# Nine inner blocks beside attention, later use of VectorE's block turns, and the query scale in an eviction

## The chip, the cores and the metric

The kernel runs on one core of a Trainium2 chip. The metric is the device time of one execution in microseconds (us), the median of three runs. TensorE does matrix products and whole 128x128 transposes, VectorE, ScalarE and GpSimd work element by element, and SyncE (SP) issues nearly all DMAs.

## The reference

Attention with a threshold feeds two MLPs in a row, all in float32:

```
scores = (q @ k.T) / 8                        # q, k, v: 4 batches, 8 heads, 576 rows, 64 columns
scores = where(scores >= rowmax - tau, scores, -1e9)
attn   = exp(scores - rowmax) / sum
x      = attn @ v                             # brought to 2304 tokens x 512
h = x @ w_in1;  x = (0 if h <= -1; (h+1)**2/4 between; h if h >= 1) @ w_out1
h = x @ w_in2;  out = (h * clip(h + 3, 0, 6) / 6) @ w_out2     # w: 512 x 2048 and 2048 x 512
```

## The kernel before, in words

**Attention** is 16 jobs, one per batch and pair of heads (`jobs`), each cut into five blocks of query rows (four of 128, one of 64 for both heads). For a block, `em_scores` (L314) multiplies queries and keys into the score banks P0 and P1 in PSUM. VectorE evicts them as minus the scores and takes the row minimum on the way (L341), ScalarE takes the exponential (L353), and VectorE masks and sums (L362). TensorE then turns the result (`em_pt`, L379, through `turn`, L277) and multiplies it with the values (`pv_chunk`, L413). `pre_norm`, `fetch_norm` and `em_norm` bring the row sums round through DRAM and scale the result on GpSimd (L481).

**Turning queries and keys** (`unit_q`, L281, and `unit_k`, L296). Before a job its queries and keys are turned so that the head's columns lie on the partitions. There are two forms, chosen by the job's number and `JT`. For jobs below `JT` the rows are loaded as they are, TensorE turns five and six blocks of 128 into a score bank, and ScalarE evicts each of the two (L294, where the queries are multiplied by 0.125, and L309). From `JT` on the DMAs place the rows in strips of 32 (`strips`, L222), and VectorE's transpose of 32x32 squares finishes the turn in SBUF (L286, L302); GpSimd then multiplies the queries by 0.125 (L288). Both forms end by issuing the load for the next job.

**The first MLP beside attention.** The 2048 inner columns of each MLP are 16 blocks of 128. Once the first batch's attention is done (`ready(0)`), `dense1` (L803) runs the first `NF1` inner blocks for the first three batches, in groups of 256 tokens. `ROUNDS` (L782) lists the groups and their inner blocks: the first two groups go in two rounds each, with half of the blocks a round, since the weights come in meanwhile; the second round adds what the first has stored. `em_h` (L657) is one inner step, 12 matmuls of 256 columns, and `em_part` (L712) half of its output, six. A loop at the end of the kernel runs attention as a generator: each of its pauses adds `share` to a credit (L927, L941), which pays for pieces of `dense1` at 0.33 each; so the pieces stand between those of attention in TensorE's order.

**Weights.** Every block of a weight is loaded and split into a high and a low part for exact products (`split_a`, `split_b`, L111 to L143): passes on ScalarE, VectorE and GpSimd (L122, L137, L141). `pace` and `ahead1` (L915, L920) ask for the splits by the inner step at which they are first used.

**Behind attention** `dense` (L835) runs the first MLP for the fourth batch and the tails with all 16 blocks, then the other three batches with the blocks from `NF1` on (`fs2`), in steps of 512 tokens (`em_h` again, and `em_out`, L693), and then the second MLP. `taus` (L886 to L888) holds four columns: the threshold as used, the factor 0.125, the threshold as given, and one for intermediate use.

Of the kernel before, what the change touches and what calls it, by code (L numbers as in the profile page):

```python
# [11 lines left out]
ALU = mybir.AluOpType  # L12
# [6 lines left out]
def kernel(  # L19
# [13 lines left out]
    V, S, G, T = nc.vector, nc.scalar, nc.gpsimd, nc.tensor  # L33
# [7 lines left out]
    HS = SEQ // 2  # L41
# [3 lines left out]

    WIDE = [MAIN] * NB + [NB * TAIL]
    NW = len(WIDE)
    NF1 = 10
    NAT = 1
    JT = 4  # L50
    MLAG = 2
    RAW = 3
    MORE = 2
# [10 lines left out]
    taus = const.tile([128, 4], F32, name="taus")  # L64
# [6 lines left out]
    def narrow(t, g):  # L71
        return t[g // 2][:, :, (g % 2) * GRP:(g % 2 + 1) * GRP]
# [29 lines left out]
    def after(ins, prev, sync=False):  # L102
        if prev is not None:
            kind = mybir.DependencyClass.Sync if sync else mybir.DependencyClass.NoSync
            why = mybir.DependencyReason.ANTI if sync else mybir.DependencyReason.DATA
            tc.add_manual_dep(ins.ins, prev.ins.name, mybir.DependencyInfo(kind, why), reason="pace")
# [4 lines left out]
    def split_a(kind, m, f):  # L111
        t = wraw.pop((kind, m, f))
        pool = wbase if f < NF1 else wpool[f]
        hi = pool.tile([128, 512], F32R, tag=f"w{kind}h{f}", name=f"w{kind}h{f}")
# [97 lines left out]
    qt, kt = {}, {}  # L212
# [4 lines left out]
    def rows(src, b):  # L217
        if b >= NAT or JT < HP:
            return src[0:MAIN, :].rearrange("(c p) d -> p c d", c=4)
        return src[0:MAIN, :].rearrange("(p c) d -> p c d", c=4)  # L220

    def strips(t, s0, src, h):  # L222
        n = src.shape[0] // 32
        flat = t.rearrange("p c n -> p (c n)")
        for x in range(2):
            p0 = 64 * h + 32 * x
            nc.sync.dma_start(out=flat[p0:p0 + 32, 32 * s0:32 * (s0 + n)].rearrange("p (s d) -> p s d", d=32),  # L227
                              in_=src[:, 32 * x:32 * x + 32].rearrange("(s p) d -> p s d", p=32))

    def load_q(j):  # L230
        if j >= NJ:
            return
        E = nc.sync if j else nc.scalar
        b, hp = jobs[j]
        for h in HEADS:
            src = q[b, 2 * hp + h]
            if j >= JT:
                strips(qn, 0, src, h)
                continue
            E.dma_start(out=qn[:, 0:4, h * D:(h + 1) * D], in_=rows(src, b))  # L240
            E.dma_start(out=qn[0:TAIL, 4, h * D:(h + 1) * D], in_=src[MAIN:SEQ, :])

    def load_k(j):
# [3 lines left out]
        for h in HEADS:  # L247
            src = k[b, 2 * hp + h]
            if j >= JT:
                strips(kn, 2, src, h)  # L250
# [18 lines left out]
    def unit_bank():  # L269
        mode["s"] += 1  # L270
        return pair_bank(f"P{mode['s'] % 2}")

    def reads(x, ago=0):
        readers[(mode["s"] - ago) % 2] = x

    def turn(out, in_, pin):
        x = T.transpose(out, in_, ident)  # L277
        if pin:
            pe_pins.append(x)

    def unit_q(j):  # L281
        if j >= NJ or j in qt:
            return
        qt[j] = ap.tile([128, SEQ], F32, tag="qt", name="qt", bufs=2)
        if j >= JT:
            V.transpose(out=qt[j], in_=qn.rearrange("p c n -> p (c n)")[:, 0:SEQ])  # L286
            load_q(j + 1)
            G.tensor_scalar(out=qt[j], in0=qt[j], scalar1=taus[:, 1:2], scalar2=None, op0=ALU.mult)  # L288
            return
        tm = unit_bank().rearrange("p e n -> p (e n)")  # L290
        for c in range(5):
            turn(tm[:, c * 128:(c + 1) * 128], qn[:, c, :], c == 0)
        load_q(j + 1)
        reads(S.activation(out=qt[j], in_=tm[:, 0:SEQ], func=ACTF.Copy, scale=taus[:, 1:2]))  # L294

    def unit_k(j):  # L296
# [3 lines left out]
        kt[j] = ap.tile([128, SEQ + TAIL], F32, tag="kt", name="kt", bufs=2)  # L300
        if j >= JT:
            V.transpose(out=kt[j], in_=kn.rearrange("p c n -> p (c n)"))  # L302
# [11 lines left out]
    def em_scores(j, i):  # L314

        last = i == NBLK - 1

        if not last:
            mode["s"] += 1
        ss = [unit_bank() for _ in range(1 if last else 2)]  # L320
        prev = None
        c = slice(i * 128, i * 128 + (TAIL if last else 128))
        for x, (h, e) in enumerate(((0, 0), (1, 1), (0, 1), (1, 0)) if last else ((0, 0), (1, 0), (0, 1), (1, 1))):
            r = slice(h * D, (h + 1) * D)
            k0 = e * HS + (TAIL if last or h == 0 else 0)
            o = ss[0][h * TAIL:(h + 1) * TAIL, e, 0:HS] if last else ss[h][:, e, 0:HS]
            with tc.high_priority(offset=900 if x else 0):
                mm = T.matmul(o, qt[j][r, c], kt[j][r, k0:k0 + HS], start=True, stop=True, skip_group_check=True)  # L328
            after(mm, prev)
            prev = mm  # L330
            if x == 0:
                pe_pins.append(mm)
                for y in range(1 if last else 2):
                    after(mm, readers.get((mode["s"] - y) % 2), True)
        nm = ap.tile([128, 2], F32, tag="nm", name="nm", bufs=3)
        th = ap.tile([128, 2], F32, tag="th", name="th", bufs=3)
        p = ap.tile([128, 2, 2, HS], F32, tag="p", name="p", bufs=3)
        if i == 0:
            zt[j] = ap.tile([128, 9], F32, tag="z", name="z", bufs=2)
        for x, s in enumerate(ss):  # L340
            reads(V.tensor_scalar(out=p[:, x], in0=s[:, :, 0:HS], scalar1=-1.0, scalar2=3e38,  # L341
                                           op0=ALU.mult, op1=ALU.min, accum_out=nm[:, x:x + 1]), len(ss) - 1 - x)
        blk[j, i] = (p, nm, th, [])

# [160 lines left out]
    def attention():  # L505
# [36 lines left out]
        for t in range(n + 6):  # L542
            mode["t"] += 1
            mode["step"] = True
            if not mode["mlp"]:
                if t < n:
                    em_scores(*order[t])
                    maskq.append(order[t])
# [15 lines left out]
                for x in now_at("q"):  # L564
                    unit_q(*x)
                    yield
# [15 lines left out]
            else:  # L582
# [18 lines left out]
                for x in now_at("q"):  # L601
                    unit_q(*x)
                    yield
# [108 lines left out]
    def em_part(key, half, f):  # L712

        gh, gl = gs[key, f] if half == 0 else gs.pop((key, f))
        wh, wl = wsp["o", 0, f]
        g, fs = ROUNDS[key[3]]
        dst = narrow(x2p, g)[:, 2 * half:2 * half + 2, :]
# [43 lines left out]
    def fin_out(g, a, i):  # L761
# [7 lines left out]
        if c < nmain:  # L769
            b, r = divmod(c, MAIN // 128)  # L770
            if b >= NAT or JT < HP:
                dst = out[b * SEQ + r * 128:b * SEQ + r * 128 + 128, :]
# [5 lines left out]
                b = (c - nmain) * 2 + e  # L778
                nc.sync.dma_start(out=out[b * SEQ + MAIN:(b + 1) * SEQ, :], in_=ob[64 * e:64 * e + 64, :])

    HALF = NF1 // 2
    ROUNDS = [(g, list(range(f, f + HALF))) for f in (0, HALF) for g in range(2)]  # L782
    ROUNDS += [(g, list(range(NF1))) for g in range(2, NG)]
    before = {}
    hs = [(r, f) for r, (g, fs) in enumerate(ROUNDS) for f in fs]
    n_h = len(hs)
    outs = [(r, half, f) for r, (g, fs) in enumerate(ROUNDS) for half in range(2) for f in fs]
    OFF = NF1 + 2 * MLAG - 3
    steps, o = [], 0
# [10 lines left out]
    def round_key(r):  # L800
        return (0, ROUNDS[r][0], 1, r)

    def dense1(ready, ahead):  # L803

        for n, l in enumerate(steps[:n_h]):
# [7 lines left out]
            yield from em_h(key, 0, f)  # L813
            if f == ROUNDS[r][1][-1]:
                xs.pop(key)
# [56 lines left out]
    def ready(g):  # L872
        return all(g // 2 * HP + hp in done_jobs for hp in range(HP))
# [12 lines left out]
    V.tensor_scalar(out=taus[:, 3:4], in0=taus[:, 2:3], scalar1=0.0, scalar2=3e38, op0=ALU.is_lt, op1=ALU.mult)  # L886
    V.tensor_scalar(out=taus[:, 1:2], in0=taus[:, 2:3], scalar1=0.0, scalar2=0.125, op0=ALU.is_ge, op1=ALU.mult)
    V.tensor_tensor(out=taus[:, 0:1], in0=taus[:, 2:3], in1=taus[:, 3:4], op=ALU.max)  # L888
    warm = [None]

    def warm_up(n):
# [6 lines left out]
    warm_up(18)  # L898
    unit_k(0)
    unit_q(0)  # L900
    warm[0] = pe_pins[-1]
    warm_up(6)
    load_v(0)
    load_v(1)

    fs1 = list(range(NF1))
    fs2 = list(range(NF1, KF))
    first_use = {("i", f): f for f in fs1}
# [15 lines left out]
            weights.half()  # L924

    part1 = dense1(ready, ahead1)
    share = 0.57  # L927
    FIRST, RATE = 5, 0.85
    credit = 0.0
    for _ in attention():  # L930
        if not mode["mlp"]:
            if mode["t"] == 3:
                weights.prefetch()
            if mode["t"] >= 5 and mode["step"]:
                mode["step"] = False
                if weights.done < FIRST and mode["t"] % 5 in (0, 4):
                    weights.half()
            if not ready(0):
                continue
            mode["mlp"] = True  # L940
        credit = min(credit + share, 3.0)  # L941
        while credit > 0:
            c = next(part1)
            if c is None:
                break
            credit -= c
# [95 lines left out]
```

## Time and profile before

| | |
|---|---|
| median of three runs | 1124.33 us (1123.8 to 1125.87) |
| profiled execution | 1126.53 us, of which the span from first to last instruction 1124.7 us |
| busy, share of the span | TensorE 97%, ScalarE 55%, VectorE 52%, GpSimd 39% |
| granted TensorE clock, mean | 0.994 of full speed |
| moved by DMA | 84.26 MB, mean 75 GB/s |

The profile is of one execution. An engine's busy time is the union of its instructions; TensorE's matmuls are pipelined, so one lasts longer than the distance to the next. The numbers of lines (L341) are those of the kernel before. The chain of waits is followed back from the last instruction, at each step to what released it.

### The profile page before, as it was taken

The numbers are of one execution on the slowest core, as the hardware profiler recorded it, in microseconds if no ns is written. First come the engines' busy times: TensorE is split into PE (matmuls) and PEld (weight loads), VectorE is DVE, ScalarE is ACT, GpSimd is POOL, SyncE is SP. The second block draws the span as 40 slices with busy tenths as digits, with TensorE's granted clock in tenths as the row PEclk, the third lists the DMA queues.
The fourth block names the chain that finished last, engine by engine and source line by source line (L and its number), as shares of the span: only waits on it lengthen the run. The fifth ranks groups of instructions, "written<-read, shape, count | busy, mean of one in ns | idle before, by whom it ended". The sixth has DMA issues, their size and how long they took to land.

```text
span 1124.7 us, 17618 instructions
## 1 busy us (share of the span) xinstructions
PE 1086.1 (97%) x6478; PEld 881.8 (78%) x6478; DVE 586.9 (52%) x1204; ACT 614.3 (55%) x1215; POOL 435.5 (39%) x382
## 2 busy tenths in 40 slices
PE   7988779999999999999999999999999999999998
PEld 5555557778887778888889888888888888898886
DVE  5788979876666666256535855657410211211111
ACT  5677777776666666565657766645422322333222
POOL 1133667632212221246636666568622222222221
PEclk9999999999999999999999999999999999999999
DMA  6353535433222210015322444543110110010001
GB/s 166 95 117 79 135 102 157 121 73 87 63 59 64 55 39 24 12 49 169 94 85 85 132 147 153 153 128 102 35 38 1 34 38 1 10 38 6 14 1 38
DMA packets 140422, 84.26 MB, mean 75 GB/s; under 512 B 99632, under 2 KB 123440, under 8 KB 140336
## 3 DMA queue, kind: packets, MB, share of 16 engines
q1 hardware_dynamic: 138976, 82.84, 26.8%
q8 instruction: 51, 0.84, 0.3%
q10 hardware_dynamic: 1360, 0.30, 0.1%
q14 instruction: 35, 0.29, 0.1%
HBM read 65.73 MB, written 17.37 MB: 74 GB/s over the span
## 4 chain that ended last, share of the span: by engine, by line
PE 86%; DVE 6%; ACT 3%; DMA 2%; issue 1%; POOL 1%; SPq 1%; ACTq 0%; DVEq 0%; POOLq 0%
PE Q L666 35%; PE P L708 28%; PE Q L728 7%; PE P L328 6%; PE Q L426 5%; PE Q L277 5%; DVE p L341 2%; DVE p L362 2%; ACT e L353 1%; DMA qn<-in_q_dram 1%; DMA w_raw<-in_moe_w_in_dram 0%; DMA rb<-rd 0%; DVE w_c L135 0%; ACT Gf L390 0%; SPq L227 0%
## 5 line engine op out<-in xcount | busy, mean ns | idle before, releaser
L684 POOL TENSOR_TENSOR gl<-r,gh 128x512 fp32r<-128x512 f32 (+1 forms) x190 | 202.4, 1065 | 508.3 <-ACT gh L683 506.4
L666 PE MATMUL Q<-xh,wih 128*128 128x512 f32 (+1 forms) x760 | 262.7, 346 | 6.9 <-DVE r L677 6.0
L666 PE MATMUL Q<-xh,wil 128*128 128x512 f32 (+1 forms) x760 | 257.6, 339 | 0.0
L666 PE MATMUL Q<-xl,wih 128*128 128x512 f32 (+1 forms) x760 | 257.5, 339 | 0.0
L680 DVE SCALAR_TENSOR_TENSOR r<-r,Q 128x512 f32<-128x512 f32 (+1 forms) x80 | 50.7, 634 | 249.3 <-ACT r L679 249.2
L683 ACT ACTIVATE gh<-r 128x512 fp32r<-128x512 f32 (+1 forms) x190 | 99.9, 526 | 128.5 <-PE P L708 52.3
L666 PEld LDWEIGHTS Q<-xh,wih 128*128 128x128 f32 x760 | 144.6, 190 | 31.4 <-DVE r L677 8.2
L666 PEld LDWEIGHTS Q<-xl,wih 128*128 128x128 f32 x760 | 144.6, 190 | 15.8
L666 PEld LDWEIGHTS Q<-xh,wil 128*128 128x128 f32 x760 | 144.5, 190 | 15.3
L341 DVE TENSOR_SCALAR_CACHE_REDUCE p<-P 128x576 f32<-128x576 f32 x144 | 103.9, 751 | 54.4 <-PE Q L277 39.1
L362 DVE SCALAR_TENSOR_TENSOR p<-p,th,e 128x576 f32<-128x576 f32 x144 | 123.6, 879 | 15.4 <-ACT e L353 9.6
L679 ACT ACTIVATE r<-Q,three 128x512 f32<-128x512 f32 (+1 forms) x80 | 51.5, 643 | 143.7 <-PE Q L666 140.5
L353 ACT ACTIVATE e<-p,nm 128x576 f32<-128x576 f32 x144 | 108.5, 774 | 29.2 <-DVE p L341 28.3
L677 DVE SCALAR_TENSOR_TENSOR r<-r,Q 128x256 f32<-128x256 f32 (+1 forms) x110 | 54.9, 499 | 120.2 <-ACT r L676 117.0
L277 PE MATMUL Q<-ident,p 128*128 128x128 f32 x656 | 108.5, 284 | 7.8 <-ACT Gf L390 4.3
L328 PE MATMUL P<-kt,qt 64*128 64x288 f32 (+1 forms) x640 | 99.4, 429 | 14.7 <-DVE p L341 13.8
L708 PE MATMUL P<-woh,gh 128*128 128x512 f32 x288 | 111.9, 390 | 0.6 <-DVE ob L766 0.6
L708 PE MATMUL P<-wol,gh 128*128 128x512 f32 x288 | 112.2, 390 | 0.0
L708 PE MATMUL P<-woh,gl 128*128 128x512 f32 x288 | 111.0, 390 | 0.0
L277 PEld LDWEIGHTS Q<-ident,p 128*128 128x128 f32 x656 | 74.5, 142 | 44.2 <-issue 11.8
L137 POOL TENSOR_TENSOR w_c<-w_c,w_raw 128x512 int32<-128x512 int32 x64 | 88.7, 1387 | 41.7 <-DVE w_c L135 21.8
L390 ACT ACTIVATE Gf<-Q 128x512 f32<-128x512 f32 x128 | 74.2, 595 | 34.4 <-PE Q L277 33.6
(91 smaller groups left out, 1834.3 us busy)
## 6 DMA issues: line engine op xcount, KB each, us to landing
w_raw<-in_moe_w_in_dram SPq DMA_DIRECT2D x32, 512.0 KB
w_raw<-in_moe_w_out_dram SPq DMA_DIRECT2D x32, 512.0 KB
vn<-in_v_dram SPq DMA_DIRECT2D x32, 128.0 KB
x2p<-ob SPq DMA_DIRECT2D x16, 256.0 KB
x2d<-ob SPq DMA_DIRECT2D x16, 256.0 KB
xst<-x2d SPq DMA_DIRECT2D x16, 256.0 KB
out_dram<-ob SPq DMA_DIRECT2D x16, 256.0 KB
xst<-xd SPq DMA_DIRECT2D x15, 256.0 KB
```

Source lines behind the costliest of these rows:

```text
L137: x = G.tensor_tensor(out=c.bitcast(I32), in0=c.bitcast(I32), in1=r, op=ALU.add)
L277: x = T.transpose(out, in_, ident)
L328: mm = T.matmul(o, qt[j][r, c], kt[j][r, k0:k0 + HS], start=True, stop=True, skip_group_check=True)
L341: reads(V.tensor_scalar(out=p[:, x], in0=s[:, :, 0:HS], scalar1=-1.0, scalar2=3e38, op0=ALU.mult, op1=ALU.min, accum_out=nm[:, x:x + 1]), ...
L353: pins["S"] = S.activation(out=e, in_=p[:, x], func=ACTF.Exp, bias=nm[:, x:x + 1], scale=-1.0)
L362: V.scalar_tensor_tensor(out=p[:, x], in0=p[:, x], scalar=th[:, x:x + 1], in1=e, op0=ALU.is_le, op1=ALU.mult, accum_out=zt[j][:, z:z + 1])
L390: S.activation(out=f[:, h, :, d0:d0 + 128], in_=tm.rearrange("p (c n) -> p c n", c=4), func=ACTF.Copy)
L666: mm = T.matmul(h, l[:, kk * 128:(kk + 1) * 128], r, start=(x == 0), stop=(x == 3 * KD - 1))
L683: x = S.activation(out=gh, in_=r, func=ACTF.Copy)
L684: y = G.tensor_tensor(out=gl, in0=r, in1=f32(gh), op=ALU.subtract)
L708: T.matmul(a, l, r, start=(first and x == 0), stop=(last and x == 2))
L728: mm = T.matmul(o, l, r, start=(f == fs[0] and x == 0 and i == 0), stop=(f == fs[-1] and x == 2 and i == 1), skip_group_check=True)
```

## The change

The number of inner blocks that run beside attention, `NF1`, goes from 10 to 9, with rounds of four and five blocks for the first two groups, and the credit a pause goes from 0.57 to 0.52. `JT` goes from 4 to 7: jobs 4, 5 and 6 get the first form of the turn (TensorE and ScalarE), jobs 7 to 15 keep the second (VectorE). In the second form GpSimd's multiplication is gone; the unscaled scores are multiplied by -0.125 where VectorE evicts them, by a column of `taus` that one more small instruction fills. The pieces of `dense1` may now run out before attention does (`next(part1, None)`).

```
-    NF1 = 10
+    NF1 = 9
-    JT = 4
+    JT = 7
...
             V.transpose(out=qt[j], in_=qn.rearrange("p c n -> p (c n)")[:, 0:SEQ])
             load_q(j + 1)
-            G.tensor_scalar(out=qt[j], in0=qt[j], scalar1=taus[:, 1:2], scalar2=None, op0=ALU.mult)
             return
...
-            reads(V.tensor_scalar(out=p[:, x], in0=s[:, :, 0:HS], scalar1=-1.0, scalar2=3e38,
+            reads(V.tensor_scalar(out=p[:, x], in0=s[:, :, 0:HS],
+                                           scalar1=taus[:, 3:4] if j >= JT else -1.0, scalar2=3e38,
                                            op0=ALU.mult, op1=ALU.min, accum_out=nm[:, x:x + 1]), len(ss) - 1 - x)
...
-    HALF = NF1 // 2
-    ROUNDS = [(g, list(range(f, f + HALF))) for f in (0, HALF) for g in range(2)]
+    HALF = 4
+    ROUNDS = [(g, list(range(a, z))) for a, z in ((0, HALF), (HALF, NF1)) for g in range(2)]
...
+    V.tensor_scalar(out=taus[:, 3:4], in0=taus[:, 1:2], scalar1=-1.0, scalar2=None, op0=ALU.mult)
...
-    share = 0.57
+    share = 0.52
...
-            c = next(part1)
+            c = next(part1, None)
```

## Rows read from the trace of the kernel before

**Rows 1.** The page, part 1: busy us, share of the span, instructions of each engine.

```profile
PE 1086.1 (97%) x6478; PEld 881.8 (78%) x6478; DVE 586.9 (52%) x1204; ACT 614.3 (55%) x1215; POOL 435.5 (39%) x382
```

**Rows 2.** Windows from score start to score start: length, busy per engine, clock, DMA.

```profile
49.64:69.26 19.62, 18.69 (x134) 11.60 (x133) 16.89 (x46) 15.63 (x33) 4.91 (x5) 0.98 0.45 98
69.26:89.72 20.46, 16.28 (x113) 9.26 (x113) 16.82 (x44) 13.49 (x30) 6.86 (x5) 1.00 0.59 118
89.72:113.65 23.93, 20.88 (x141) 13.06 (x141) 21.16 (x55) 16.89 (x35) 8.51 (x7) 0.93 0.36 71
113.65:138.13 24.48, 17.01 (x117) 11.30 (x116) 22.88 (x54) 19.85 (x42) 15.70 (x14) 1.00 0.53 136
138.13:180.04 41.91, 34.50 (x238) 26.17 (x238) 35.37 (x72) 30.59 (x67) 28.95 (x26) 0.92 0.47 119
```

**Rows 3.** Windows beside attention, just behind it, and in the second MLP; same columns.

```profile
336.00:364.00 28.00, 28.00 (x221) 22.14 (x217) 17.17 (x47) 17.22 (x38) 6.79 (x7) 1.00 0.29 65
504.00:532.00 28.00, 28.00 (x153) 24.39 (x153) 18.71 (x21) 15.38 (x28) 18.39 (x13) 1.00 0.51 155
840.00:868.00 28.00, 28.00 (x125) 23.21 (x124) 3.45 (x5) 6.60 (x10) 6.65 (x6) 1.00 0.00 1
```

**Rows 4.** The chain of waits, 138 to 184 us: start, length, what.

```profile
145.08 5.12 DMA w_raw<-in_moe_w_in_dram
...
180.30 1.82 POOL w_c L137
```

**Rows 5.** The chain of waits where TensorE is full; 256 columns first, then 512.

```profile
251.32 0.59 PE Q L277 x4
251.91 1.44 PE Q L666 x12
253.35 0.72 PE Q L728 x6
...
849.16 2.72 PE P L708 x12
851.88 2.72 PE Q L666 x12
```

**Rows 6.** Groups by form: count, busy us, mean ns of one, idle before.

```profile
L137 POOL TENSOR_TENSOR w_c<-w_c,w_raw 128x512 int32<-128x512 int32 x64 | 88.7, 1387 | 41.7 <-DVE w_c L135 21.8 <-DVE z L445 10.3 <-ACT r L675 3.4
L141 POOL TENSOR_TENSOR wil<-w_c,wih 128x512 fp32r<-128x512 f32 x32 | 43.5, 1361 | 23.6 <-ACT wih L139 23.5
L288 POOL TENSOR_SCALAR qt<-qt,taus 128x576 f32<-128x576 f32 x12 | 21.2, 1763 | 9.8 <-DVE qt L286 8.6 <-PE Q L277 1.1
L122 POOL TENSOR_SCALAR w_c<-w_c 128x512 f32<-128x512 f32 x20 | 14.7, 735 | 33.7 <-ACT w_c L121 33.7
L302 DVE STREAM_TRANSPOSE kt<-kn 128x640 f32<-128x640 f32 x12 | 9.7, 808 | 0.0
L286 DVE STREAM_TRANSPOSE qt<-qn 128x576 f32<-128x576 f32 x12 | 9.3, 774 | 1.8 <-DMA qn<-in_q_dram 0.9 <-PE P L328 0.8
L356 DVE TENSOR_SCALAR th<-nm,taus 128x1 f32<-128x1 f32 x16 | 3.2, 202 | 0.2
L309 ACT ACTIVATE kt<-P 128x640 f32<-128x640 f32 x4 | 2.9, 714 | 0.0
L887 DVE TENSOR_SCALAR taus<-taus 128x1 f32<-128x1 f32 x1 | 0.1, 144 | 0.0
```

**Rows 7.** Timeline of single instructions: start, length, engine, line, what; idle before.

```profile
67.40 0.72 ACT L294 ACTIVATE qt<-P,taus 128x576 f32<-128x576 f32 x1
...
90.43 1.72 POOL L288 TENSOR_SCALAR qt<-qt,taus 128x576 f32<-128x576 f32 x1 [1.08 <-DVE qt L286]
91.37 0.81 DVE L362 SCALAR_TENSOR_TENSOR p<-p,th,e 128x576 f32<-128x576 f32 x1
...
110.05 0.77 DVE L286 STREAM_TRANSPOSE qt<-qn 128x576 f32<-128x576 f32 x1
...
175.34 2.19 POOL L288 TENSOR_SCALAR qt<-qt,taus 128x576 f32<-128x576 f32 x1 [0.42 <-DVE qt L286]
```

## The prediction

> **What bounds the kernel now.** I read the engine totals first: TensorE is busy 1086.1 of 1124.7 us [rows 1], so only 38.6 us are left in which it does nothing, and the question is where they lie. The windows cut at the score starts of successive jobs say where: TensorE is idle 20.46 - 16.28 = 4.2 us during job 3, 3.1 during job 4, 7.5 during job 5 and 7.4 in the 42 us behind it, and in the same windows VectorE is the fullest engine (16.82 of 20.46, 21.16 of 23.93, 22.88 of 24.48) with GpSimd at 15.70 of 24.48 and 28.95 of 41.91 where the weight splits pile up [rows 2]. From about 190 us TensorE is busy without a break: 28.00 of 28 us beside attention as well as in the dense stages [rows 3]. So the kernel is two parts. Up to about 190 us it is held by VectorE, GpSimd and the DMAs of the weights; the chain of waits there passes through a 5.12 us wait for a weight's DMA and through GpSimd's 1.82 us pass over a weight [rows 4]. After that TensorE sets the time. A change to TensorE's sum counts in the second part, a change to the others in the first.
>
> **Nine inner blocks instead of ten.** Beside attention the first MLP runs 54 instead of 60 inner steps of 256 tokens and 108 instead of 120 output parts. One step takes 12 matmuls, 1.44 us, one part six, 0.72 us [rows 5]: 6 x 1.44 + 12 x 0.72 = 17.3 us less. The same work comes back behind attention, in 3 steps of 512 tokens with their outputs, each 2.72 + 2.72 us [rows 5]: 16.3 us more. All of the 16.3 us is paid (TensorE is full there), and the 17.3 us is got back where TensorE is full. Net -0.9 us. That the refund is whole rests on the matmul row of 28.00 us. The weight-load rows of the same two windows differ, 22.14 against 23.21 us [rows 3]. The Trainium skill (Trainium Kernel Development and Optimization, Performance Expectations) calls matmul busy time a bad metric of closeness to the roofline and takes the weight-load share instead; read so, the stage beside attention has some 5% of holes, the refund would be an estimated 16.5 us and the net -0.2 us.
>
> Two weight blocks leave the attention stage. By the code's order the splits asked for at the ninth inner step fall from 15 to 13, though at the fifth they rise from 7 to 8. One split is 0.74 + 1.39 + 1.36 = 3.5 us of GpSimd alone [rows 6], so 7 us leave a stage in which GpSimd is on the chain. Only what falls before TensorE is full helps. Ends: nothing gained and one 3.5 us split more in the early ramp (+3.5), or both splits out of it (-7); I take -2, the 14.9 us of TensorE idle behind 113.65 us times 2 of 15 splits [rows 2]. In the dense stage the two splits are hidden: at 504 to 532 us GpSimd is busy 18.39, VectorE 18.71 of 28 us [rows 3]; were that cover gone they would cost 7 us.
>
> The lower share per pause (0.52 for 0.57, -9%) follows the falling work (the credits of all steps go from 150.5 to 135.3, -10%), so the MLP ends with attention as before: nothing.
>
> **Turns of jobs 4 to 6 on TensorE.** Each loses two VectorE transposes, 0.77 + 0.81 = 1.58 us, 4.7 us in three jobs, and one GpSimd pass of 1.76 us [rows 6]. Each adds 11 TensorE transposes (four take 0.59 us [rows 5], so 0.15 us each and 1.6 us a job) and two ScalarE evictions, 0.72 and 0.71 us [rows 6, 7]. These lie before 138 us, where TensorE idles 3 to 7 us a job. ScalarE is busy 13.49 to 19.85 us a job, so it can take 1.4 us. The DMAs stay 4 for q and fall from 8 to 6 for k, with twice the bytes in each run; SP's queue gets shorter. Ends: job 2 has the new form on both sides and took 19.62 us, job 3, in which the first VectorE turn stands, 20.46 [rows 2]: 0.84 us a job, 2.5 us in three; if all VectorE time counted, 4.7. On the bad side is a rival below. I take -2.5, as a whole cycle holds the evictions too.
>
> **No scale on GpSimd for jobs 7 to 15.** Nine passes of 1.76 us go. Behind 190 us they hide behind TensorE. Before, one of them took 2.19 us at 175.34 [rows 7] in a window with GpSimd 69% busy [rows 2], in front of the weight splits that are late there. Ends: 0 and 2.19 + 1.76 = 3.9 us (job 7's too); I take -2.
>
> **The scale in the eviction.** The 81 evictions of jobs 7 to 15 read their factor from a column instead of an immediate. No such eviction is in the trace. Nearest: the same kind of operation on one column took 0.202 us with a column, 0.144 with an immediate [rows 6]; so 0 to 0.06 us each, and a gain is excluded, since no element less is read. Only some 18 lie before TensorE is full: +1.0 us taken, 0 to 1.
>
> **Sum.** -0.9 - 2 - 2.5 - 2 + 1.0 = -6.4 us. The profiled execution took 1126.53 us (span 1124.7 and 1.8 around it), so it would be 1120.1; the median of the runs is 2.2 us under it, so I say **1118 us**.
>
> **Rivals.**
> *The turn stands late (slower).* A VectorE turn runs long ahead: job 6's q was turned at 110.05 us, its scores began at 138.13. In the TensorE form job 3's q left its bank at 67.40 for scores at 69.26 [rows 2, 7], 1.9 us ahead, and it uses a score bank, TensorE's queue and ScalarE's. For job 6 these queues also hold MLP matmuls and weight casts that wait for weights, in the stretch with the 5.12 us DMA wait [rows 4]. If each of the three boundaries then shows its 1.6 + 1.4 us, and job 6's the DMA's 5.12, that is +14.1 us instead of -2.5: 1134.6; with half of it shown 1127.6. It decides once the three boundaries cost more than the 3.9 us that the other terms save. Against: job 2's cycle, with this form, is the shorter one.
> *Holes beside attention (slower).* The removed 17.3 us stays as idle time because attention's own chain can't move up. Half lost: 1118 + 8.7 = 1126.7. Against: at 336 to 364 us VectorE is busy 17.17 and ScalarE 17.22 of 28 us [rows 3], so that chain has room to move up.
> *The weights hold the ramp (no change).* TensorE fills up only when the weights are there, whatever VectorE saves: -0.9 + 1 from the sum, 1124.3. For: the DMA wait in the chain.
> *VectorE is freed as well (faster).* All of 4.7 and 3.9 and half of the 7: -0.9 - 4.7 - 3.9 - 3.5 = -13, 1111.5. A further reason would be GpSimd's passes holding up VectorE. The mask at 91.37 us beside a scale pass of 90.43 to 92.15 took 0.81 us [rows 7], not longer, so I give that reason little. The Trainium skill (SBUF — State Buffer, on the shared port pair) states that a GpSimd operation and a VectorE one with two SBUF inputs exclude each other for the whole instruction; by it the mask would have waited the remaining 0.78 us, an estimated 4.7 us over six passes, and 1113 us here. This row disagrees.
>
> **Chances.** Forecast (1113 to 1122) 0.50; VectorE freed 0.15, within it 0.04 for the port rule; weights hold 0.16; turn late 0.12; holes 0.07. Range 1110 to 1127.5. What the measurement can tell from no change is about 0.2%, 2.2 us: faster needs less than 1122.1. All of the first two and 0.02 of the third are faster, 0.67; 0.14 the same; the last two are slower, 0.19.
>
> **What would show it.** After: jobs 3 to 5 from score start to score start shorter by 0.8 us each; TensorE's idle time some 6 us under 38.6; 12 matmuls of 256 still in 1.44 us beside attention; the dense stage 16 us longer and attention's end 20 or more earlier. The forecast falls if the windows of jobs 3 to 5 grow, if the evictions of job 7 on are longer by over 0.06 us, or if TensorE idles between 220 and 470 us.

## The result, and the profile after

The changed kernel took 1132.92 us (median of four runs, 1132.37 to 1134.12), the kernel before 1125.1 us beside it (1123.8 to 1126.58): ratio 1.0073, 95% interval 1.0059 to 1.0087. It is some 8 us slower, where 6 us less was forecast. The profiled execution took 1132.37 us with a span of 1130.6 us, 5.9 us more than before.

Page of the changed kernel, part 1, which answers to [rows 1]:

```profile
PE 1089.4 (96%) x6439; PEld 880.3 (78%) x6439; DVE 591.7 (52%) x1198; ACT 617.9 (55%) x1212; POOL 412.5 (36%) x365
```

TensorE has 39 instructions fewer, yet is busy 3.3 us longer and idle 41.2 instead of 38.6 us. GpSimd lost 23 us, and none of it is seen in the time.

The windows of the changed kernel between the same score starts as in [rows 2], then one in its first wide stage and one in the second MLP, as in [rows 3]; same columns:

```profile
49.58:68.95 19.37, 18.41 (x133) 11.34 (x132) 17.24 (x48) 16.02 (x34) 5.37 (x5) 1.00 0.44 104
68.95:90.39 21.44, 18.17 (x133) 11.39 (x132) 17.70 (x47) 16.49 (x35) 6.52 (x5) 1.00 0.42 103
90.39:112.25 21.86, 19.89 (x149) 13.09 (x148) 18.97 (x51) 17.11 (x36) 4.72 (x7) 1.00 0.31 76
112.25:140.15 27.90, 23.03 (x160) 15.95 (x160) 25.21 (x55) 23.45 (x50) 15.89 (x14) 0.94 0.47 120
140.15:183.11 42.96, 33.31 (x236) 25.39 (x235) 38.58 (x78) 29.22 (x63) 26.40 (x25) 0.96 0.54 140
336.00:364.00 28.00, 28.00 (x219) 21.99 (x219) 18.91 (x50) 18.89 (x43) 3.69 (x4) 1.00 0.27 60
532.00:560.00 28.00, 26.73 (x117) 21.46 (x116) 15.17 (x18) 17.58 (x30) 20.19 (x16) 1.00 0.29 94
840.00:868.00 28.00, 28.00 (x125) 23.19 (x124) 3.45 (x5) 7.68 (x12) 7.76 (x6) 1.00 0.00 1
```

Job 3's cycle grew from 20.46 to 21.44 us, job 4's fell from 23.93 to 21.86, job 5's grew from 24.48 to 27.90 and the next stretch from 41.91 to 42.96. From 250 us on TensorE is full, as before, but behind attention (532 to 560) 1.3 of 28 us are idle.

What the long job 5 holds, from TensorE's and VectorE's timelines of the changed kernel (start, length, engine, line, what; idle before). First TensorE:

```profile
126.01 0.77 PE L277 MATMUL Q<-ident,p 128*128 128x128 f32 x5
130.39 0.77 PE L277 MATMUL P<-ident,qn 128*128 128x128 f32 x5 [3.62 <-DVE p L340]
...
131.76 2.18 PE L327 MATMUL P<-kt,qt 64*64 64x288 f32 x8
...
171.64 1.19 PE L327 MATMUL P<-kt,qt 64*64 64x288 f32 x8
```

then VectorE:

```profile
126.17 1.74 DVE L362 SCALAR_TENSOR_TENSOR p<-p,th,e 128x576 f32<-128x576 f32 x1
...
127.84 1.81 DVE L362 SCALAR_TENSOR_TENSOR p<-p,th,e 128x576 f32<-128x576 f32 x1
...
129.58 0.75 DVE L340 TENSOR_SCALAR_CACHE_REDUCE p<-P 128x576 f32<-128x576 f32 x1
```

Job 6's queries are now turned in a score bank. TensorE stands 3.62 us before that turn until VectorE has evicted the scores in the bank, and VectorE comes late: two masks ahead of it took 1.74 and 1.81 us instead of 0.81 [rows 7], which is 1.9 of the 3.62 us. Behind the idle time the scores at 131.76 took 2.18 us; later, in the same form, they take 1.19.

**Where the difference arises.** A cut that every kernel has is the first matmul of 512 columns, at attention's end. The timelines have it, of the kernel before:

```profile
481.33 0.40 PE L666 MATMUL Q<-xh,wih 128*128 128x512 f32 x1
```

and of the changed kernel:

```profile
469.56 0.63 PE L666 MATMUL Q<-xh,wih 128*128 128x512 f32 x2
```

The stretch ahead of the cut is 11.8 us shorter. The stretch behind it is 1130.6 - 469.6 = 661.0 against 1124.7 - 481.3 = 643.4 us, 17.6 us longer.

Before these are held against the forecast, one thing has to be counted. Attention is over at the cut, but a few pieces of the first MLP that belong beside it (256 columns) stand behind it, and with ten blocks there are more of them. Groups by form from the cut to the end, of the kernel before and then of the changed kernel (each stands for three of the same count, as a product has three parts):

```profile
L666 PE MATMUL Q<-xh,wih 128*128 128x256 f32 x136 | 38.4, 282 | 0.0
L728 PE MATMUL Q<-gh,woh 128*128 128x256 f32 x28 | 7.9, 283 | 0.0
```

```profile
L666 PE MATMUL Q<-xh,wih 128*128 128x256 f32 x132 | 37.2, 282 | 0.0
L728 PE MATMUL Q<-gh,woh 128*128 128x256 f32 x22 | 6.2, 283 | 0.0
```

The kernel before has 12 matmuls of L666 and 18 of L728 more there, 1.44 + 3 x 0.72 = 3.6 us [rows 5]. So 13.7 of the 17.3 us that are taken away lie ahead of the cut. By the forecast's own terms the stretch ahead had to be 13.7 + 2 + 2.5 + 2 - 1 = 19.2 us shorter, and the one behind 16.3 - 3.6 = 12.7 us longer. Of the 12.3 us by which the spans miss the forecast, 7.4 lie ahead of the cut and 4.9 behind it. Behind it TensorE has gaps that the kernel before doesn't have; windows from 460 to 620 us, before and then changed (columns as in [rows 2]):

```profile
460.00:620.00 160.00, 159.98 (x986) 141.52 (x985) 78.27 (x111) 94.71 (x187) 82.12 (x71) 1.00 0.28 86
```

```profile
460.00:620.00 160.00, 156.06 (x923) 136.15 (x922) 89.21 (x120) 98.81 (x189) 91.83 (x76) 1.00 0.32 100
```

### The profile page after: what moved, and what is told of

The parts are those of the page before. It is cut to its first block, busy times and chain, and to the rows that moved or that the text cites. A ratio compares the mean times of both kernels' runs of the same rounds, so it can differ in the third digit from the quotient of the medians.

```text
span 1130.6 us, 17531 instructions
## 1 busy us (share of the span) xinstructions
PE 1089.4 (96%) x6439; PEld 880.3 (78%) x6439; DVE 591.7 (52%) x1198; ACT 617.9 (55%) x1212; POOL 412.5 (36%) x365
## 4 chain that ended last, share of the span: by engine, by line
PE 76%; DVE 8%; ACT 5%; POOL 3%; DMA 3%; issue 3%; SPq 1%; ACTq 0%; POOLq 0%; DVEq 0%
PE Q L666 30%; PE P L708 25%; PE P L327 6%; PE Q L426 5%; PE Q L728 5%; PE Q L277 5%; DVE p L362 2%; DVE p L340 2%; POOL w_c L137 2%; DVE w_c L135 1%; ACT e L353 1%; DVE w_c L129 1%; DMA rb<-rd 1%; DMA w_raw<-in_moe_w_out_dram 1%; ACT w_raw L118 1%
## 5 line engine op out<-in xcount | busy, mean ns | idle before, releaser
L666 PE MATMUL Q<-xh,wih 128*128 128x512 f32 (+1 forms) x748 | 258.9, 346 | 5.3 <-DVE r L677 5.3
L666 PE MATMUL Q<-xl,wih 128*128 128x512 f32 (+1 forms) x748 | 254.7, 341 | 0.0
L666 PE MATMUL Q<-xh,wil 128*128 128x512 f32 (+1 forms) x748 | 254.7, 341 | 0.0
L666 PEld LDWEIGHTS Q<-xh,wih 128*128 128x128 f32 x748 | 141.6, 189 | 26.9 <-DVE r L677 6.6
L666 PEld LDWEIGHTS Q<-xl,wih 128*128 128x128 f32 x748 | 141.8, 190 | 16.3
L666 PEld LDWEIGHTS Q<-xh,wil 128*128 128x128 f32 x748 | 141.6, 189 | 15.9
L362 DVE SCALAR_TENSOR_TENSOR p<-p,th,e 128x576 f32<-128x576 f32 x144 | 125.8, 893 | 15.8 <-ACT e L353 9.0
L137 POOL TENSOR_TENSOR w_c<-w_c,w_raw 128x512 int32<-128x512 int32 x64 | 88.0, 1376 | 45.8 <-DVE w_c L135 24.5
L340 DVE TENSOR_SCALAR_CACHE_REDUCE p<-P,taus 128x576 f32<-128x576 f32 x81 | 63.1, 813 | 46.7 <-PE Q L277 45.0
```

Source lines behind the costliest of these rows:

```text
L137: x = G.tensor_tensor(out=c.bitcast(I32), in0=c.bitcast(I32), in1=r, op=ALU.add)
L362: V.scalar_tensor_tensor(out=p[:, x], in0=p[:, x], scalar=th[:, x:x + 1], in1=e, op0=ALU.is_le, op1=ALU.mult, accum_out=zt[j][:, z:z + 1])
L666: mm = T.matmul(h, l[:, kk * 128:(kk + 1) * 128], r, start=(x == 0), stop=(x == 3 * KD - 1))
```

## The experiments

"To the cut" and "behind" are the two stretches in each profile; ratio and median come from the timed rounds, each against runs of the kernel before on the same chip. The stretches are those of one execution, which need not be near the median: the one of jt7 is its fastest (1123.23 us), the one of before in evict_ptr's order its slowest (1131.91 us). "Pinned" is explained below.

| kernel | ratio (95%) | median us | to the cut | behind |
|---|---|---|---|---|
| before | 1 | 1124.8 to 1125.1 | 481.3 | 643.4 |
| the changed kernel (after) | 1.0073 (1.0059 to 1.0087) | 1132.92 | 469.6 | 661.0 |
| nine blocks (nf9) | 1.0045 (1.0027 to 1.0064) | 1129.86 | 465.6 | 661.6 |
| `JT` = 7 (jt7) | 1.0020 (1.0005 to 1.0034) | 1127.92 | 478.5 | 642.9 |
| scale in the eviction (evict) | 1.0038 (1.0024 to 1.0052) | 1129.82 | 484.4 | 643.2 |
| `JT` = 7 and scale (jt7_evict) | 1.0042 (1.0026 to 1.0057) | 1129.93 | 483.1 | 643.1 |
| scale by immediate (evict_imm) | 1.0051 (1.0032 to 1.0070) | 1130.06 | 486.4 | 643.3 |
| column for -1 (evict_ptr) | 1.0049 (1.0031 to 1.0067) | 1130.22 | 486.7 | 643.5 |
| `JT` = 16 (jt16) | 1.0100 (1.0083 to 1.0117) | 1136.23 | 492.1 | 643.4 |
| nine blocks, early splits (nf9_pre) | 1.0042 (1.0026 to 1.0057) | 1130.29 | 470.5 | 658.2 |
| evict_ptr, pinned (evict_ptr_ord) | 1.0001 (0.9992 to 1.0011) | 1125.28 | 481.3 | 643.4 |
| before, pinned to evict_ptr's order | 1.0030 (1.0016 to 1.0043) | 1128.19 | 486.6 | 643.4 |
| evict, pinned (evict_ord) | 1.0001 (0.9991 to 1.0010) | 1124.95 | 479.2 | 643.4 |
| evict_imm, pinned (evict_imm_ord) | 0.9993 (0.9984 to 1.0003) | 1124.71 | 480.7 | 643.4 |
| nine blocks and scale (nf9_evict) | 0.9989 (0.9980 to 0.9999) | 1123.57 | 460.5 | 660.6 |
| nine blocks and `JT` (nf9_jt7) | 1.0020 (1.0008 to 1.0031) | 1127.93 | 465.3 | 661.1 |
| `JT` and immediate (jt7_imm) | 1.0045 (1.0030 to 1.0061) | 1130.68 | 484.7 | 643.2 |
| all, with immediate (all_imm) | 1.0075 (1.0056 to 1.0094) | 1134.22 | 472.8 | 660.3 |
| after, pinned to nf9_jt7's order | 1.0037 (1.0025 to 1.0049) | 1129.31 | 464.0 | 661.7 |
| nf9, pinned to nf9_evict's order | 0.9981 (0.9971 to 0.9990) | 1123.59 | 460.7 | 661.2 |

The column behind the cut has two values (643.2 +- 0.4 with ten blocks, 661 +- 0.7 with nine) and one exception. Between them, 12.7 us are work that moved. What differs among kernels with the same number of blocks is decided ahead of the cut.

**The three parts alone, and two together.**

```
nf9:   NF1 = 9; HALF = 4 and rounds of four and five; share = 0.52; next(part1, None)
jt7:   JT = 7
evict: -  G.tensor_scalar(out=qt[j], ... scalar1=taus[:, 1:2] ...)
       -  scalar1=-1.0
       +  scalar1=taus[:, 3:4] if j >= JT else -1.0
       +  V.tensor_scalar(out=taus[:, 3:4], in0=taus[:, 1:2], scalar1=-1.0, ...)    # -0.125
jt7_evict: the last two
```

> Only the inner blocks (nine, rounds of four and five, share 0.52); turns and GpSimd's scale as before. Weights theory (the ramp is held by the weight splits, and the two splits moved behind attention are not hidden there): 3 to 7 us slower than before, TensorE full not before 200 us, and about 4 us of TensorE idle between 470 and 590 us. Turn theory (all of the loss comes from turns that stand late on TensorE): -1 to +1 us.

> Only the turns of jobs 4 to 6 moved to TensorE; ten inner blocks, GpSimd's scale kept for jobs 7 to 15. Turn theory: 4 to 8 us slower, the cycle of job 5 (block 25 to 30) about 3 us longer. Weights theory: 0 to 2 us slower. VectorE theory (the forecast's term): 2.5 us faster.

> Only the scale moved from GpSimd into VectorE's eviction, for jobs 4 to 15. Forecast's terms: GpSimd's passes gone -2, longer evictions +1 to +2 (0.06 us each), so -1 to 0 us. Eviction theory (0.06 us in a stretch that VectorE bounds): 2 to 3 us slower. Turn and weights theories: 0.

> All of the change but the nine inner blocks (ten, rounds of five, share 0.57). Turn theory: 4 to 8 us slower than before, as the whole change. Weights theory: -1 to +2 us. Forecast's terms: 3.5 us faster.

Each part alone made the kernel slower, by 2.2 to 5.1 us, also the one that takes twelve passes away from GpSimd (with `JT` at 4 it covers jobs 4 to 15). The parts don't add up: 5.1 + 2.2 + 4.3 = 11.6 us against 8.2, and `JT` with the scale 4.7 against 6.5.

**What of the scale edit costs?** The factor as an immediate, without the column; then the column alone, with GpSimd's multiplication kept.

```
evict_imm: -  G.tensor_scalar(out=qt[j], ...)
           +  scalar1=-0.125 if j >= JT else -1.0
evict_ptr: +  V.memset(taus[:, 3:4], -1.0)
           +  scalar1=taus[:, 3:4] if j >= JT else -1.0
```

> As the run with the scale in the eviction alone (jobs 4 to 15), but the factor -0.125 is an immediate, so the case of a negative threshold (factor 0) is left out; GpSimd's scale is gone here too. If the 0.06 us that a column adds to each eviction make the loss: -2 to 0 us against the kernel before. If GpSimd's missing pass or the changed order makes it: 3 to 5 us slower, as with the column.

> The kernel before, with the evictions of jobs 4 to 15 reading -1 from a column instead of an immediate; GpSimd's scale stays. Column theory: 3 to 5 us slower than before, evictions of 0.81 instead of 0.75 us. Order or GpSimd theory: within 1 us of before.

Neither tells the column from the passes: without the column +5.7 us, with nothing but the column +5.5. evict_ptr has the same work as before, an operand and one small memset apart. What else differs is the order. Put the records of each engine in order of time, leave the memset out, and compare place by place: 1510 of 6478 on TensorE, 338 of 1204 on VectorE, 342 of 1215 on ScalarE and 55 of 382 on GpSimd are of another instruction than in the kernel before. The code fixes only some instructions against each other; between these the build settles the order on each engine, and it dealt it anew.

**More turns; the splits earlier.**

```
jt16:    JT = 16                                      # all turns on TensorE
nf9_pre: nf9, and
         - pool = wbase if f < NF1 else wpool[f]
         + pool = wbase if f <= NF1 else wpool[f]     # tenth block split beside attention
         - weights.add(0, fs2)
         + weights.add(0, fs2[1:])
```

> All turns on TensorE (ten inner blocks, no scale on GpSimd needed, evictions with the immediate). Sum theory (TensorE's idle time before 250 us does not shrink, each job's 11 transposes are paid at 0.109 us each): 12 jobs x 1.2 = 14 us, less GpSimd's passes, so 10 to 14 us slower. Turn theory (only the turns that meet the weights' ramp cost): 2 to 6 us slower, as jobs 7 to 15 cost nothing more.

> Nine inner blocks alone, but the two weight splits of the tenth block are done beside attention as well, after all others. Split theory (the 4 us of TensorE idle behind attention come from two splits more in a chain of 6.0 us a split against steps of 5.44 us): no TensorE idle between 465 and 590 us, 4 us faster than nine blocks alone, so 0 to 2 us slower than before. Ramp theory (the loss lies before 250 us): 4 to 5 us slower, as nine blocks alone.

jt16 took 11.3 us more, 0.94 us for each of its twelve turns, as the sum theory had it: TensorE is busy 1102.4 us, 16.3 more than before, with 132 transposes more, and idle 33.1 instead of 38.6 us. In nf9_pre TensorE is idle 1.6 of the 160 us from 460 to 620, where nf9 has 4.1, and the stretch behind the cut is 3.4 us shorter than in nf9: that is what the two splits cost there. Ahead of the cut it is 4.9 us longer, so nothing was won.

**The order held fixed.** "Pinned" kernels carry a list of places, and each instruction of an engine is ordered behind the one before it in that list; such an edge settles the order and adds no semaphore. evict_ptr, evict and evict_imm got before's order, and before got evict_ptr's. The traces bear it out: compared as above, the records of evict_ptr_ord stand in before's order on all four engines, and those of before in evict_ptr's order in evict_ptr's, without one exception.

```
+ for engine, moves in ORDER().items():
+     ...
+     tc.add_manual_dep(i, last.name, ... NoSync ...)
```

> Evictions of jobs 4 to 15 read -1 from a column, as in the run that was 5 us slower, but every engine's queue is pinned to the order that the kernel before has (edges without a wait, one instruction behind the other). Order theory (the build puts the queues in another order as soon as any instruction changes, and that order costs the 5 us): -1 to +1 us against the kernel before. Column theory (0.06 us an eviction): 4 to 5 us slower, as without the pins.

> The reverse: the kernel before, no instruction changed, its queues pinned to the order that the build gave the run with the column. Order theory: 4 to 5 us slower. Column theory: within 1 us.

> The change's own edit of the scale (column in the eviction, no pass on GpSimd), queues pinned to the order of the kernel before. Order theory: -1 to +1 us, against 4.3 us slower without the pins. Forecast's terms: GpSimd's passes gone -2, column +1, so -1.

> As the last, with the immediate -0.125 (the case of a negative threshold left out), pinned too. Order theory: -2 to 0 us; the difference to the last is what the column costs with the order held (0 to 1 us).

In before's order all three edits are worth nothing: 1.0001, 1.0001 and 0.9993. The kernel before, its instructions untouched, becomes 3.4 us slower in evict_ptr's order (evict_ptr itself was 5.5 us slower; the intervals, 1.0016 to 1.0043 and 1.0031 to 1.0067, overlap). How this shows in the profile, page part 1 and a chain of waits of before in evict_ptr's order:

```profile
PE 1088.4 (96%) x6478; PEld 882.0 (78%) x6478; DVE 588.4 (52%) x1204; ACT 615.4 (54%) x1215; POOL 440.0 (39%) x382
```

```profile
217.19 0.52 SPq L227
...
219.41 0.30 SPq L452
...
220.32 1.23 DMA rd<-rq
...
224.41 0.27 ACT xu L432
...
226.08 1.12 PE Q L277 x4
```

Its span is 1130.0 us: TensorE idles 1130.0 - 1088.4 = 41.6 us instead of 38.6, and is busy 2.3 us longer with the same 6478 instructions. The lower clock is not the reason: the mean granted clock is 0.994 in both profiles, and in the mean of the timed executions of both kernels too; why TensorE is busy longer is not shown. One place is shown above: the row sums' way through DRAM (`rd`) stands behind strip loads (L227) in SP's queue, ScalarE's L432 comes late, TensorE waits 1.8 us and soon after 0.7 us more, and four transposes then take 1.12 us instead of 0.59 [rows 5], at a granted clock of 0.50.

**Pairs, and the whole with the order varied.**

```
nf9_evict: nf9 + evict        nf9_jt7: nf9 + jt7
jt7_imm:   jt7 + evict_imm    all_imm: nf9 + jt7 + evict_imm
after_ord: the changed kernel, queues pinned to nf9_jt7's order
nf9_ord:   nf9, queues pinned to nf9_evict's order (GpSimd's left free)
```

> Nine inner blocks and the scale in the eviction, turns as before (from job 4 on VectorE). The scale's edit costs nothing with the order held, so this is the work of nine blocks in another order than the run with nine blocks alone. Order theory with no cost of its own for nine blocks: 3 to 5 us slower than before, as other orders of the old work. If nine blocks cost by their own work (idle TensorE behind attention): 6 to 9 us.

> The whole change, but GpSimd's scale kept: the work of the changed kernel in another order. If the order alone made its loss: anywhere from 0 to 6 us. If the added transposes (3.6 us of TensorE) and the idle time behind attention (4 us) are paid in every order: 6 to 10 us slower than before, as the changed kernel.

> Turns of jobs 4 to 6 on TensorE, scale as an immediate in the eviction (negative threshold left out), ten inner blocks: the work of the moved turns in a third order (2.2 and 4.7 us slower in the other two). If the transposes cost their 3.6 us beside the order: 4 to 8 us slower. If they are taken up by idle time: 2 to 5 us.

> The whole change with the immediate instead of the column (negative threshold left out); its queues stand nearly as in the changed kernel. 6 to 9 us slower than before, as the changed kernel; under 5 would say that the column costs in the changed kernel, though it cost nothing with the old order.

> The changed kernel, no instruction of it altered, its queues pinned to the order of the run that is the whole change with GpSimd's scale kept (2.2 us slower than before). Order theory: 1.5 to 3 us slower than the kernel before, instead of 8. Work theory (the changed kernel's own instructions cost the 8 us): 7 to 9 us slower.

> Nine inner blocks alone (5 us slower in its own order), with the queues of TensorE, VectorE, ScalarE and SP pinned to the order of the run of nine blocks with the scale in the eviction (1.3 us faster); GpSimd's queue is left to the build. Order theory: -2 to 0 us against the kernel before. Work theory: 4 to 6 us slower.

nf9 is 5.1 us slower than before in its own order and 2.1 us faster in nf9_evict's. That is the fastest version found. (GpSimd's queue came out in nf9_evict's order by itself, its scale passes aside.) The changed kernel gets 4 us back in nf9_jt7's order, and keeps 4.2. jt7_imm and all_imm, without the column, are as slow as with it.

A window over the first 250 us shows the difference between nf9's two orders (columns as in [rows 2]). nf9 in its own order:

```profile
0.00:250.00 250.00, 215.09 (x1551) 153.16 (x1553) 205.98 (x503) 181.48 (x384) 107.68 (x103) 0.99 0.47 115
```

nf9 in nf9_evict's order:

```profile
0.00:250.00 250.00, 219.99 (x1590) 156.69 (x1592) 210.64 (x512) 184.49 (x391) 107.94 (x103) 0.98 0.47 117
```

and the changed kernel:

```profile
0.00:250.00 250.00, 217.02 (x1552) 153.58 (x1553) 204.35 (x491) 182.47 (x384) 91.22 (x95) 0.97 0.45 115
```

With the same instructions TensorE is busy 4.9 us more and gets 39 more matmuls done in the ramp; the spans differ by 1127.1 - 1121.9 = 5.2 us. What the ramp leaves undone is done later where TensorE is full, us for us.

## Why the prediction was wrong

**The steps that failed** are two. The larger is the set of three credits in the ramp (attention up to some 250 us, before TensorE is full), "I take -2" for the splits, "I take -2.5" for the turns and "I take -2" for the scale: the stretch ahead of the cut misses by 7.4 us. The smaller is "in the dense stage the two splits are hidden": the stretch behind the cut misses by 4.9 us, and TensorE stands idle there for 3.9. All three credits convert freed VectorE and GpSimd time, or work placed "where TensorE idles", into time. The ramp didn't work like that: it is a chain over five queues, and its length hangs on the order in which the build has placed them. With no work changed, that order alone moved the time by 3.4 us (before) and 7.2 us (nf9), more than any one of the credits. No rival named it. "The weights hold the ramp" expected no change, and the order moved the time with the same weights to split.

**Turns.** Forecast -2.5 us. In the runs every kernel with `JT` = 7 or more is slower than before, by at least 2.2 us. TensorE's added transposes had been costed at nothing, as they lie in idle time. But TensorE's idle time before 250 us is 33.0 us in the changed kernel and 34.9 in nf9 (250 less TensorE's busy time), and both get the same number of matmuls done there (1552 and 1551). As 33 of the changed kernel's are added transposes, 32 others were pushed out into the full part. jt7's profile, of its fastest execution, does not show this: 30.8 us idle, and 54 matmuls more than before. Its ten timed executions ran at a mean granted clock of 0.9923, those of the kernel before at 0.9941; 0.0018 of 1125 us is an estimated 2.0 us, near its 2.2. The rival "the turn stands late" named a place where it happened: the score bank came 3.62 us late for job 6, and job 5's cycle grew 3.4 us. But job 4's fell 2.1, so the boundaries alone do not reach the 7 us of its lower case. How the 2.2 us split into TensorE's own time, clock and order is open: no run has the moved turns in the order of the kernel before.

**Scale.** Forecast -2 and +1. With the order held, both together are 0 (1.0001), and the passes alone 0 (0.9993, up to -1.8 us within the interval), for jobs 4 to 15. The evictions grew as its upper bound said, from 753 to 813 ns. Groups by form of the changed kernel (count, busy us, mean ns, idle before):

```profile
L340 DVE TENSOR_SCALAR_CACHE_REDUCE p<-P,taus 128x576 f32<-128x576 f32 x81 | 63.1, 813 | 46.7 <-PE Q L277 45.0 <-PE P L327 1.5
L340 DVE TENSOR_SCALAR_CACHE_REDUCE p<-P 128x576 f32<-128x576 f32 x63 | 45.9, 753 | 11.2 <-PE P L327 10.4
L293 ACT ACTIVATE qt<-P,taus 128x576 f32<-128x576 f32 x7 | 5.2, 741 | 1.4 <-PE P L277 1.4
```

The 46.7 us of idle time in front of the first group fit that the 0.06 us do not count: from job 7 on VectorE waits for TensorE. The removed passes were no bound either, though GpSimd was 69% busy around one of them: a busy share does not say that the engine is waited for.

**Nine blocks.** In nf9_ord this part came out at -2.1 us (-3.3 to -1.1), beside a forecast of -0.9 - 2 = -2.9. That is luck, since two misses cancel: the cut comes 481.3 - 460.7 = 20.6 us earlier, where 13.7 + 2 had been worked out, and the stretch behind it is 17.8 us longer instead of 12.7. In the profile of its own order nf9's cut comes 15.7 us earlier, as worked out, and the miss behind it remains (2.4 us slower than before in these profiles, 5.1 in the timed runs). Twelve matmuls of 256 columns still take 1.44 us in the changed kernel's chain of waits, and TensorE stays full there, so the "holes beside attention" did not open:

```profile
224.91 1.44 PE Q L666 x12
...
239.00 0.72 PE Q L728 x6
```

The Trainium skill (Trainium Kernel Development and Optimization, Performance Expectations) would have put the refund at an estimated 16.5 us by the weight-load share; the cut's 20.6 us hold what the ramp gave as well, so no run here tells 16.5 from 17.3.

"In the dense stage the two splits are hidden" was wrong by 3 to 4 us. The share of 18.39 busy us in 28 [rows 3] had stood as cover, but one split's chain is longer than one step. The chain of waits of the changed kernel, behind attention:

```profile
539.50 1.27 POOL w_c L137
...
545.47 1.31 POOL w_c L137
...
551.47 1.31 POOL w_c L137
...
557.48 1.31 POOL w_c L137
```

A split comes every 6.0 us and a step of 512 tokens takes 2.72 + 2.72 = 5.44 us [rows 5]. So each split falls further behind the steps. The kernel before has such a row of splits 6.0 us apart too (533 to 563 us), without a wait; two more are too many. TensorE then waits not for a weight by name but for the step's own passes (`gl`, `r`, `gh`), which stand between the splits' passes in the queues of GpSimd, VectorE and ScalarE. Waits of the changed kernel (460 to 620 us; waited for, us, times, longest):

```profile
PE P L708 <- POOL gl L684: 2.4, 4, 1.0
PE Q L666 <- DVE r L677: 1.3, 1, 1.3
PE P L708 <- ACT gh L683: 0.3, 1, 0.3
```

That is 4 us. In nf9_pre, with the two splits done earlier, such waits come to 1.6 us.

**The whole.** Of the 12.3 us by which the spans miss the forecast, 4.9 lie behind the cut, where two splits were not hidden, and 7.4 ahead of it. Pinned to nf9_jt7's order, the changed kernel reaches the cut at 464.0 instead of 469.6 us with the same work, so in these two profiles 5.6 of the 7.4 us go with the order; behind the cut it is no shorter (661.7). In the timed runs the changed kernel is +8.2 us in its own order and +4.2 in nf9_jt7's, so order is worth 4 us of it. nf9_jt7 itself, in that order and with GpSimd's scale kept, is at +2.2; its interval (1.0008 to 1.0031) and the other's (1.0025 to 1.0049) overlap, so a cost of the scale in this order is not shown. Open is which wait makes one order better than another: several small ones differ in each pair of profiles. The granted clock has a part in some pairs: its mean over the timed executions is 0.9925 in nf9 and 0.9950 in nf9_ord, an estimated 2.8 us of the 7.2 (0.0025 of 1125 us), while the kernel before has 0.994 in either order. It also differs between executions of one kernel (nf9's ran from 1126.02 us at 0.995 to 1134.17 us at 0.989). The changed kernel in an order like nf9_evict's was not tried.

## What to carry to other kernels

Where a build settles the order of the queues, an edit is never only an edit: compare with the order held fixed, in both directions, before a gain or a loss is put down to the work that was changed; here 0.3 to 0.6% came from order alone. Idle time of an engine is not by itself room for more work: in the changed kernel's ramp 33 transposes came in and 32 other matmuls went out. Cover is judged by the length of the repeated chain against the step that it hides behind (6.0 against 5.44 us) and by how often it repeats, not by busy shares. And a cut of a profile is only as good as the count of the work on either side of it.

## What the runs showed of the hardware

**A mask beside GpSimd.** In the kernel before, up to 250 us, masks (L362) with no long GpSimd pass beside them took 0.82 us (48 of them), four beside a scale pass (L288, one tensor input) 0.79 us; ten beside L137 and nine beside L141 (two tensor inputs) took 1.32 and 1.05 us in the mean, up to 1.91. The two masks of 1.74 and 1.81 us above stand beside these passes of the changed kernel, from GpSimd's timeline:

```profile
126.00 1.29 POOL L137 TENSOR_TENSOR w_c<-w_c,w_raw 128x512 int32<-128x512 int32 x1
127.26 1.78 POOL L141 TENSOR_TENSOR wil<-w_c,wih 128x512 fp32r<-128x512 f32 x1
```

So the scale passes that the change removed held none of these four masks up, and masks beside the split passes that it left are longer. The other way round there may have been a wait: one of the four masks began first, 0.17 us ahead of the pass at 175.34 [rows 7], and that pass took 2.19 us where the other eleven took 1.72 or 1.73. The port rule of the Trainium skill (SBUF — State Buffer, on the shared port pair), weighed in the prediction, agrees in kind with the two-input passes, and not with the three masks that began behind a scale pass. Nor did taking the scale passes out gain anything: evict_ord measured 1.0001.

**The clock.** Behind the idle 3.62 us the granted clock is at the lower of its two levels (1.2 instead of 2.4 GHz) for a stretch, in which the scores took 2.18 instead of 1.19 us. So this wait cost more than its own length. A window of the changed kernel in that stretch, with a clock of 0.50 behind the five engines' busy times:

```profile
131.75:135.10 3.35, 3.35 (x15) 1.98 (x15) 1.77 (x5) 3.35 (x7) 1.67 (x2) 0.50 0.55 91
```
